# First MLP by sevens: second product ordered by the rows' arrival, rests of rows put off, second MLP's first weights split sooner, its block sums on DVE

## The chip, the cores and the metric

One core of one Trainium2 chip runs the kernel. The metric is the device time of one execution in microseconds (us), taken as the median of several runs. Engines are named as in the profile: PE (TensorE matmul), PEld (its weight load), DVE (VectorE), ACT (ScalarE), POOL (GpSimd), SP (the queue from which transfers are issued).

## What is computed

Three stages follow one another. Linear attention (4 batches, 8 heads, 576 tokens, head size 64) with a normalisation of each head; its result is a matrix x of 2304 rows and 512 columns. The first MLP has three first products whose maximum is taken. The second MLP has four experts whose results are weighted and added.

```python
def _moe_ref(x, w1, w2, w3, w_out):            # w1..w3: 512 x 768, w_out: 768 x 512
    h = np.maximum(np.maximum(x @ w1, x @ w2), x @ w3)
    return (h @ w_out).astype(np.float32)

def _moe2_ref(x, domain_probs, w1, w2):        # 4 experts, w1: 512 x 1024, w2: 1024 x 512
    p = domain_probs / (domain_probs.sum(-1, keepdims=True) + 1e-09)
    for e in range(E):
        h = np.maximum(x @ w1[e], 0.0)
        out += p[:, e:e + 1] * (h @ w2[e])
```

## The kernel before

**Split numbers.** TensorE multiplies fp32r. Every fp32 operand is kept as two fp32r parts: `hi` (a rounded copy, made by ACT) and `lo` (the rest, source minus `hi`, made by DVE in `low`, L504). A product is three matmuls, hi by hi, hi by lo and lo by hi.

**Row blocks and sevens.** The 2304 rows are six blocks of T = 384. The first MLP does block 0 and the first product of block 1 plainly (`moe1_a`, `moe1_o`). From then on two blocks go together, and a product of a 2 by 2 arrangement of blocks is done with seven block products instead of eight (`seven`, L580; six matmuls of 384 columns each). The block sums that this needs are made beforehand: `w1_sums` on the weights (four subtractions, POOL), `y_sum` on the rows (four sums, numbered 0 to 3, of 128 x 768). `w1_split`, `t_split` and `y_split` then make hi and lo of the result.

**Banks of a product.** The seven products k = 0..6 use two PSUM banks only, in the order A X A X A A X. After products 0, 2 and 4 ACT copies bank A; after 1, 4 and 6 DVE adds that copy to bank X; after 5 bank A is read again. The next product on a bank waits until it has been read.

**First MLP, units.** `units` (L620) are 18: two pairs of blocks (sb = 1, 2), three pairs of columns of the hidden layer (p), three weights (i). In a unit DVE takes the running maximum in `mx` (L661, L667), and in the last unit of three (i = 2) ACT writes the hi part of the hidden rows (L670); the lo part is handed back by `after_product1` and made by `low`. Four parts of hidden rows h[a, blk] result, in the order (0,0) after product 1, (1,1) after 4, (0,1) after 5 and (1,0) after 6. Their second product (`second1`, 48 matmuls) fills the gaps between the products of the next three units; `FILL` says how many matmuls follow each product. A block's sums with `blk` = 1 go through two banks in turn (4 and 5, evacuated by DVE L700 or ACT), those of `blk` = 0 stay in banks 0 to 3. `t_load` fetches a unit's weights two units ahead (kept in DRAM, `w_d`), POOL makes their sums, `t_split(0)` and `t_split(1)` split them after products 3 and 5 of the unit before.

**When a rest is made.** `low` puts the subtraction into a list; `lag_end` after the next product works the list off, and once more after product 5 of a unit.

**Second MLP, rounds.** 48 rounds: expert e, pair of blocks sb (3), pair of hidden columns pr (4). A round is seven products and, between them, 36 matmuls of 512 columns of the round before (`second`, L715); `store` (DVE L732) adds a finished tile to the sum. The weights of an expert are loaded, summed and split during the last four rounds of the expert before; the first expert's begin in the last units. The rows of the next pair are loaded after product 4 of pr = 0, their sums are made on POOL in pr = 1 (`y_sums`), their splits in pr = 3. In round 0 the last second product of the first MLP is the filling (`FILL_18`).

**Order.** The first stage follows a list written out by hand, `steps`: of its letters A is one product of three of block 0 or 1 with its maximum, H a split of hidden rows, P a second product, E the copies of block 0's result, Y one sum of rows, V one split of rows, R one half of `t_split`. Engines work off their queues in program order; so does SP.

## Time and profile before

| | |
|---|---|
| median of 3 runs | 1144.63 us (1143.02 to 1144.75) |
| profiled execution | 1143.08 us, its span 1141.3 us |
| PE busy | 1108.7 us, 97% of the span, 6020 matmuls |
| DVE, ACT, POOL busy | 652.8, 428.7, 274.5 us (57%, 38%, 24%) |
| mean granted TensorE clock | 0.995 of full speed |

The span is the time from the first to the last instruction. Busy time of PE counts a matmul from its start to its modelled end, and consecutive ones overlap. "Idle before" an instruction is put down to the releaser that came last.

### The profile page before, as it was taken

To read this page: it belongs to the slowest core of one execution; us is meant where nothing else is said; L and a number is where in the kernel's file an instruction comes from. 1 tells how busy PE (TensorE), PEld (TensorE's weight loads), DVE (VectorE), ACT (ScalarE), POOL (GpSimd) and SP (SyncE) were. 2 spreads that over 40 slices of the span, in tenths; PEclk is the share of its full clock that TensorE was granted. 3 is DMA by queue.
4 is the path that set the end of the run, shared out by engine and by line. 5 is a ranking of instruction groups with operands and counts; after the bars stand their busy time and mean duration, and the time that the engine had idled before them with its cause. 6 is when DMAs were issued, how large, how long until landed. Compare 5 with 4: busy or idle time off the path is not lost.

```text
span 1141.3 us, 15399 instructions
## 1 busy us (share of the span) xinstructions
PE 1108.7 (97%) x6020; PEld 1014.0 (89%) x6020; DVE 652.8 (57%) x981; ACT 428.7 (38%) x772; POOL 274.5 (24%) x244
## 2 busy tenths in 40 slices
PE   7889999999998999999999999999999999999998
PEld 6789998999998989889989888998998898999887
DVE  3889986567557564245744436583535466343523
ACT  2553233434433445243644233452424254332321
POOL 1346632422333130205220202412020522001000
PEclk9999999999999999999999999999999999999999
DMA  9945544211411412014140403432030625040111
GB/s 260 295 146 168 152 166 149 71 56 49 156 56 56 148 56 81 31 50 138 63 175 1 166 1 130 129 120 102 28 139 6 216 65 194 1 149 19 47 64 56
DMA packets 89257, 118.49 MB, mean 104 GB/s; under 512 B 11616, under 2 KB 57696, under 8 KB 89184
## 3 DMA queue, kind: packets, MB, share of 16 engines
q1 hardware_dynamic: 88480, 117.17, 32.2%
q8 instruction: 47, 0.77, 0.3%
q10 hardware_dynamic: 704, 0.33, 0.1%
q14 instruction: 26, 0.21, 0.1%
HBM read 87.59 MB, written 29.88 MB: 103 GB/s over the span
## 4 chain that ended last, share of the span: by engine, by line
PE 79%; DVE 11%; DMA 4%; ACT 2%; issue 2%; SPq 1%; POOL 1%; DVEq 0%; POOLq 0%; ACTq 0%
PE bank L586 40%; PE bank L715 35%; PE bank L683 3%; DMA w_da<-cv_a 1%; DVE ts L507 1%; DVE cv_a L232 1%; DVE ss L345 1%; DMA v<-in_v_dram 1%; DVE hr L507 1%; DVE xt L365 1%; DVE fa L659 1%; DVE fa L661 1%; DMA k<-in_k_dram 1%; DVE cv_a L235 1%; DMA w1s<-w_da 1%
## 5 line engine op out<-in xcount | busy, mean ns | idle before, releaser
L527 POOL TENSOR_TENSOR w1s<-w1s 128x256 f32<-128x256 f32 x136 | 117.1, 880 | 384.4 <-DMA w1s<-in_moe_w_dram 219.2
L611 DVE TENSOR_TENSOR fa<-bank,fa 128x384 f32<-128x384 f32 x144 | 80.1, 557 | 207.8 <-ACT fa L608 118.3
L715 PE MATMUL bank<-wr,hr 128*128 128x512 f32 x720 | 197.3, 393 | 0.0
L562 POOL TENSOR_TENSOR fa<-fa 128x768 f32<-128x768 f32 x44 | 88.4, 2020 | 289.1 <-DMA fa<-y_d 227.6
L586 PE MATMUL bank<-xr,wr 128*128 128x384 f32 x756 | 153.4, 338 | 0.0
L715 PEld LDWEIGHTS bank<-wr,hr 128*128 128x128 f32 x720 | 133.6, 188 | 17.8
L586 PEld LDWEIGHTS bank<-xr,wr 128*128 128x128 f32 x756 | 136.0, 188 | 9.7
L586 PE MATMUL bank<-rb,wr 128*128 128x384 f32 x696 | 141.3, 337 | 2.0 <-DVE hr L594 1.0
L608 ACT ACTIVATE fa<-bank 128x384 f32<-128x384 f32 x144 | 70.6, 490 | 189.8 <-PE bank L586 189.0
L586 PEld LDWEIGHTS bank<-rb,wr 128*128 128x128 f32 x696 | 125.1, 188 | 12.0 <-DVE hr L594 1.5
L715 PE MATMUL bank<-wl,hr 128*128 128x512 f32 x360 | 102.9, 394 | 0.1
L715 PE MATMUL bank<-wr,xr 128*128 128x512 f32 x288 | 93.9, 393 | 0.0
L586 PE MATMUL bank<-rb,wl 128*128 128x384 f32 x384 | 78.9, 342 | 2.4 <-DVE fa L659 2.4
L594 DVE SCALAR_TENSOR_TENSOR hr<-fa,hr 128x384 fp32r<-128x384 f32 x72 | 54.5, 757 | 42.6 <-ACT hr L593 42.6
L586 PEld LDWEIGHTS bank<-rb,wl 128*128 128x128 f32 x384 | 68.9, 190 | 7.6 <-DVE fa L659 4.0
L715 PEld LDWEIGHTS bank<-wl,hr 128*128 128x128 f32 x360 | 66.7, 188 | 9.0 <-issue 0.4
L715 PE MATMUL bank<-wr,rb 128*128 128x512 f32 x216 | 69.0, 393 | 0.0
L593 ACT ACTIVATE hr<-fa 128x384 fp32r<-128x384 f32 x72 | 37.8, 525 | 80.5 <-DVE fa L611 80.5
L593 ACT ACTIVATE xr<-fa 128x384 fp32r<-128x384 f32 x48 | 25.2, 525 | 103.1 <-DVE fa L611 103.1
L715 PEld LDWEIGHTS bank<-wr,xr 128*128 128x128 f32 x288 | 53.9, 188 | 7.9
L659 DVE TENSOR_TENSOR fa<-bank,fa 128x384 f32<-128x384 f32 x54 | 29.9, 553 | 51.0 <-ACT fa L656 36.7
L507 DVE TENSOR_TENSOR rb<-fa,rb 128x768 fp32r<-128x768 f32 (+1 forms) x45 | 43.5, 966 | 25.5 <-ACT rb L571 23.5
(170 smaller groups left out, 1789.6 us busy)
## 6 DMA issues: line engine op xcount, KB each, us to landing
fa<-y_d SPq DMA_DIRECT2D x24, 768.0 KB, 6.7
stage_a<-in_moe_w_dram SPq DMA_DIRECT2D x18, 512.0 KB, 4.1
w1s<-w_da SPq DMA_DIRECT2D x36, 256.0 KB, 2.8
o_d<-fa SPq DMA_DIRECT2D x36, 256.0 KB, 3.9
fa<-o_d SPq DMA_DIRECT2D x36, 256.0 KB, 5.3
w1s<-in_moe_w_dram SPq DMA_DIRECT2D x32, 256.0 KB, 3.1
w2s<-in_moe_w_dram SPq DMA_DIRECT2D x32, 256.0 KB, 3.2
w_da<-cv_a SPq DMA_DIRECT2D x18, 256.0 KB, 4.7
```

Of the source, the lines that this page charges most:

```text
L232: nc.vector.scalar_tensor_tensor(out=ti, in0=words[:, :, 0], scalar=29, in1=ti, op0=ALU.logical_shift_right, op1=ALU.bitwise_or)
L507: nc.vector.tensor_tensor(out=lo, in0=src, in1=f32(hi), op=ALU.subtract)
L527: eng.tensor_tensor(out=st[:, o], in0=st[:, a], in1=st[:, b], op=ALU.subtract)
L562: eng.tensor_tensor(out=y_part(o), in0=y_part(a), in1=y_part(b), op=op)
L586: nc.tensor.matmul(out, w[wi][:, c * P : (c + 1) * P], y[yi][:, c, :], start=(i == 0 and k in BEGIN), stop=(i == 5), skip_group_check=k no ...
L593: nc.scalar.activation(out=h[0], in_=src, func=AF.Relu)
L594: nc.vector.scalar_tensor_tensor(out=h[1], in0=src, scalar=0.0, in1=f32(h[0]), op0=ALU.max, op1=ALU.subtract)
L608: nc.scalar.activation(out=s[k // 2], in_=a, func=AF.Copy)
L611: nc.vector.tensor_tensor(out=t, in0=x, in1=t, op=ALU.add)
L659: nc.vector.tensor_tensor(out=mx[done] if i == 0 else t, in0=x, in1=t, op=ALU.add)
L683: nc.tensor.matmul(bank[:, :T], w[:, wi, c * P : (c + 1) * P], h[a, blk][hi], start=((blk == 1 or p == 0) and a == 0 and n == 0), stop=((b ...
L715: nc.tensor.matmul(banks[i], h[a, i // TPB][hi][:, i % TPB * P : (i % TPB + 1) * P], w[a][wi], start=(pr == 0 and a == 0 and m == 0), stop ...
```

## The change

The second product of the first MLP takes its parts in another order: all of (blk 0, a 0), then blk 1, then (blk 0, a 1). A rest of hidden rows is made 2 to 4 products later instead of one (`by`), through a list with due times (`lag_at`). In a unit `t_split(1)` stands ahead of `after_product1` at product 5. The first sums of rows stand earlier in `steps`. The second MLP's first weights (e = 0, pr = 0) have a place of their own (`w1e`) and are loaded in unit 10, summed in unit 12 on POOL and split in units 13 and 15, instead of loaded in unit 16 and split in unit 17; the next ones (pr = 1) take the load in unit 16. In the second MLP the four sums of rows go from POOL (pr = 1) to DVE (pr = 2, one after each of products 0 to 3). The copies of the last block 4 are all on ACT, and `FILL_18` is redistributed. Rests in round 0 are put off by a product as well.

```diff
--- before.py
+++ after.py
@@ -431,7 +431,7 @@
     def y_put(j, c, bank, t):
-        if c % 2:
+        if c % 2 and j < 4:
             nc.vector.tensor_copy(out=t, in_=bank)
         else:
             nc.scalar.activation(out=t, in_=bank, func=AF.Copy)
@@ -463,14 +463,14 @@
     FILL = [(0, 2, 1, 2, 2, 5, 2, 2), (0, 2, 1, 2, 2, 5, 2, 2), (0, 2, 1, 2, 2, 5, 2, 2)]
     FILL_0 = [(0, 0, 1, 0, 1, 4, 1, 1)] * 3
     FILL_9 = [(0, 4, 4, 3, 3, 4, 2, 2), (0, 1, 2, 1, 2, 4, 2, 1), (0, 1, 2, 1, 2, 4, 2, 1)]
-    FILL_18 = (0, 8, 6, 6, 6, 8, 7, 7)
+    FILL_18 = (0, 8, 8, 10, 10, 6, 3, 3)
     SPLIT = {(8, 1): (0,), (8, 2): (1,), (8, 4): (2,), (8, 6): (3,), (0, 0): (4,), (0, 2): (5,), (0, 3): (6,)}
     bank_of = {"A": banks[7], "X": banks[6]}
     wr = []
     late = {}
-    lag = [None]
+    lag = {"now": None, "put": []}
     first = [1]
     def y_at(k):
@@ -501,35 +501,45 @@
         return first, second
-    def low(lo, src, hi):
-
-        if lag[0] is None:
+    def low(lo, src, hi, by=1):
+
+        if lag["now"] is None:
             nc.vector.tensor_tensor(out=lo, in0=src, in1=f32(hi), op=ALU.subtract)
         else:
-            lag[0].append((lo, src, hi))
-
-    def lag_end(again=None):
-        put, lag[0] = lag[0] or [], None
-        for p in put:
-            low(*p)
-        lag[0] = again
-
-
-    def w1_load(e, pr):
-        st = late["w1"].rearrange("p (n c f) -> p n c f", n=8, f=P)
+            lag["put"].append((lag["now"] + by, (lo, src, hi)))
+
+    def lag_at(now):
+
+        put, lag["put"], lag["now"] = lag["put"], [], None
+        for due, args in put:
+            if now is None or due <= now:
+                low(*args)
+            else:
+                lag["put"].append((due, args))
+        lag["now"] = now
+
+
+    def w1_at(early):
+
+        if early:
+            return late["w1e"], part(fa, 7 * HK + 3 * T, 4 * 2 * P)
+        return late["w1"][:, : 4 * 2 * P], late["w1"][:, 4 * 2 * P :]
+
+    def w1_load(e, pr, early=False):
+        st = w1_at(early)[0].rearrange("p (n c f) -> p n c f", n=4, f=P)
         for at, f in ((0, pr + NPR), (2, pr)):
             src = e_w1[e, :, f * P : (f + 1) * P].rearrange("(c p) f -> p c f", p=P)
             nc.sync.dma_start(out=st[:, at : at + 2].rearrange("p n c f -> p (n c) f"), in_=src)
-    def w1_sums(eng):
-        st = late["w1"].rearrange("p (n f) -> p n f", n=8)
+    def w1_sums(eng, early=False):
+        st = [t[:, n * 2 * P : (n + 1) * 2 * P] for t in w1_at(early) for n in range(4)]
         for o, a, b in ((4, 0, 2), (5, 1, 4), (6, 1, 0), (7, 3, 5)):
-            eng.tensor_tensor(out=st[:, o], in0=st[:, a], in1=st[:, b], op=ALU.subtract)
-
-    def w1_split(pr, half):
+            eng.tensor_tensor(out=st[o], in0=st[a], in1=st[b], op=ALU.subtract)
+
+    def w1_split(pr, half, early=False):
         cols = slice(0, 3 * 2 * P) if half == 0 else slice(3 * 2 * P, 7 * 2 * P)
         (hi, lo), _ = w_slot(pr)
-        src = late["w1"][:, 2 * P :][:, cols]
+        src = w1_at(early)[half][:, 2 * P if half == 0 else 0 :]
         nc.scalar.activation(out=hi[:, cols], in_=src, func=AF.Copy)
         low(lo[:, cols], src, hi[:, cols])
@@ -673,19 +683,19 @@
     def second1(sb, p):
         h = h_of((sb - 1) * NPF + p + 1)
-        for blk in (1, 0):
-            for c in range(KD):
-                bank = banks[4 + c % 2] if blk else banks[c]
-                for a in range(2):
-                    w = wt["o", 0, p + a * NPF]
-                    for n, (wi, hi) in enumerate(((0, 0), (1, 0), (0, 1))):
-                        last = (a, n) == (1, 2)
-                        nc.tensor.matmul(
-                            bank[:, :T], w[:, wi, c * P : (c + 1) * P], h[a, blk][hi],
-                            start=((blk == 1 or p == 0) and a == 0 and n == 0),
-                            stop=((blk == 1 or p == NPF - 1) and last),
-                        )
-                        yield (blk, c) if last else None
+
+        parts = [(0, c, 0) for c in range(KD)] + [(1, c, a) for c in range(KD) for a in range(2)]
+        for blk, c, a in parts + [(0, c, 1) for c in range(KD)]:
+            bank = banks[4 + c % 2] if blk else banks[c]
+            w = wt["o", 0, p + a * NPF]
+            for n, (wi, hi) in enumerate(((0, 0), (1, 0), (0, 1))):
+                last = (a, n) == (1, 2)
+                nc.tensor.matmul(
+                    bank[:, :T], w[:, wi, c * P : (c + 1) * P], h[a, blk][hi],
+                    start=((blk == 1 or p == 0) and a == 0 and n == 0),
+                    stop=((blk == 1 or p == NPF - 1) and last),
+                )
+                yield (blk, c) if last else None
     def rest1(sb, p, blk, c):
         if blk == 0:
@@ -830,7 +840,7 @@
             "A012 A112 d13 c14 d14 A212 s12.pp A202 s13.av s14.vv A102 H12.pv c15 P1 H02 A003.v d15 c16 c17 "
             "A013 A113 d16 d17 A203 A103 s15.pp c18 A213 H03 s16.pv H13.pv d18 s17 s18.vv c19 d19 c20 d20 "
             "s19.pv A004 A014 A104 c21 s20.av c22 P2 A204 A114 d21 W H04 d22 c23 s21.pv s22.av A214 P3 "
-            "A005.v H14 A015.v d23 s23.av Z A205 P4 V0 A105 H05 R0 V1 A215 Y0 A115 H15 P5 E Y1 V3 Y2 V4 R1 "
+            "A005.v H14 A015.v d23 s23.av Z A205 Y0 P4 V0 Y1 A105 Y2 H05 R0 V1 A215 A115 H15 P5 E V3 V4 R1 "
             "Y3 V6"
         ).split()
         for st in steps:
@@ -881,6 +891,7 @@
                 cv_cm.__exit__(None, None, None)
                 lp = ctx.enter_context(tc.tile_pool(name="late", bufs=1, reuse_waits="tile"))
                 late["o"] = lp.tile([P, 2, DM], F32, name="ob")
+                late["w1e"] = lp.tile([P, 4 * 2 * P], F32, name="w1e")
                 late["w1"] = lp.tile([P, 8 * 2 * P], F32, name="w1s")
                 t_cm = tc.tile_pool(name="tp", bufs=1, reuse_waits="tile")
                 late["t"] = t_cm.__enter__().tile([P, 2 * 4 * 2 * P], F32R, name="ts")
@@ -937,25 +948,31 @@
             go(fill, first)
             for k in range(7):
                 product1(u, k)
+                if k == 5 and u + 1 < len(units):
+                    t_split(1)
                 put = after_product1(u, k)
-                lag_end([])
+                lag_at(7 * u + k)
                 if put:
-                    low(*put)
+                    low(*put, by={1: 2, 4: 3, 5: 2, 6: 4}[k])
                 go(fill, after[k])
                 if u + 1 < len(units):
                     if k == 3:
                         t_split(0)
                     if k == 5:
-                        t_split(1)
-                        lag_end([])
+                        lag_at(7 * u + 6)
                         if u + 2 < len(units):
                             t_load(u + 2)
                         else:
-                            w1_load(0, 0)
+                            w1_load(0, 1)
                         w1_sums(nc.gpsimd)
-                elif k in (1, 3):
-                    w1_split(0, k // 2)
+
+                if (u, k) == (10, 6):
+                    w1_load(0, 0, True)
+                if (u, k) == (12, 0):
+                    w1_sums(nc.gpsimd, True)
+                if (u, k) in ((13, 4), (15, 4)):
+                    w1_split(0, u // 15, True)
                 if (u, k) in ((0, 6), (9, 6)):
                     y_load(*((2, x_d) if sb == 1 else (0, None)))
                 if (u, k) == (3, 6):
@@ -966,8 +983,7 @@
                     y_sum(nc.vector, (3, 4, 6, 7).index(u % 9))
                 for n in SPLIT.get((u % 9, k), ()) if u > 7 else ():
                     y_split(n)
-        lag_end()
-        go(fill, 99)
+        assert not any(fill)
         t_cm.__exit__(None, None, None)
         late["w2"] = ctx.enter_context(tc.tile_pool(name="w2p", bufs=1, reuse_waits="tile")).tile([P, 2, DM], F32, name="w2s")
@@ -982,12 +998,13 @@
         for e in range(E):
             for pr in range(NPR):
                 n = (e * NSB - 1) * NPR + pr
-                w1_at, w2_at = (n + 1, n + 2) if e else (pr - 1, pr)
-                if w1_at >= 0:
-                    at(w1_at - 1, 3 if e else 5, w1_load, e, pr)
-                    at(w1_at - 1, 3 if e else 5, w1_sums, nc.gpsimd)
+                w1_by, w2_at = (n + 1, n + 2) if e else (pr - 1, pr)
+                if e or pr > 1:
+                    at(w1_by - 1, 3 if e else 5, w1_load, e, pr)
+                    at(w1_by - 1, 3 if e else 5, w1_sums, nc.gpsimd)
+                if e or pr:
                     for i in range(2):
-                        at(w1_at, (1 if e or pr == 1 else 4) + i, w1_split, pr, i)
+                        at(w1_by, (1 + i if e else 2 + i if pr == 1 else 4 + i), w1_split, pr, i)
                 at(w2_at - 1, 6, w2_load, e, pr)
                 for i in range(2):
                     at(w2_at, 3 + 2 * i, w2_split, pr, i)
@@ -998,7 +1015,6 @@
         before = None
         fill = second_of(*units[-1][:2])
-        run(-1, 5)
         run(-1, 6)
         go(fill, FILL_18[0])
         for n, (e, sb, pr) in enumerate(rounds):
@@ -1012,6 +1028,7 @@
                 product(pr, k)
                 after_product(n, k)
                 if n == 0:
+                    lag_at(7 * len(units) + k)
                     go(fill, FILL_18[1 + k])
                     for i in SPLIT.get((0, k), ()):
                         y_split(i)
@@ -1023,14 +1040,15 @@
                 if more:
                     if pr == 0 and k == 4:
                         y_load((sb + 1) % NSB)
-                    if pr == 1 and k == 3:
-                        y_sums(nc.gpsimd)
+                    if pr == 2 and k < 4:
+                        y_sum(nc.vector, k)
                     if pr == NPR - 1:
                         y_split(k)
                 if e and pr == 1 and k == 4:
                     o_load(sb)
                 run(n, k)
             before = (e, sb, pr)
+            lag_at(None)
         for i in second(n, pr):
             if i is not None:
                 store(e, sb, i)
```

## Rows read from the trace of the kernel before

**Rows 1.** Windows: us; busy us (x) PE, PEld, DVE, ACT, POOL; PEclk; DMA; GB/s.

```profile
176.60:367.00 190.40, 184.92 (x1023) 177.24 (x1022) 120.55 (x198) 75.72 (x144) 61.59 (x73) 1.00 0.25 80
367.00:388.50 21.50, 18.89 (x98) 18.24 (x96) 18.02 (x27) 10.77 (x19) 3.69 (x4) 0.92 0.32 110
388.50:410.00 21.50, 19.48 (x94) 16.82 (x95) 12.08 (x12) 6.83 (x13) 13.50 (x11) 1.00 0.48 158
410.00:1128.00 718.00, 718.00 (x3565) 646.14 (x3564) 354.11 (x498) 265.98 (x469) 122.64 (x90) 1.00 0.25 85
```

**Rows 2.** Waits of PE from 176.6 to 410 us: total us, times, longest.

```profile
PE bank L683 <- DVE hr L507: 3.0, 2, 2.6
PE bank L586 <- ACT fa L656: 2.6, 5, 1.1
PE bank L586 <- DVE fa L659: 2.4, 5, 0.6
PE bank L586 <- DVE hr L594: 1.0, 1, 1.0
PE bank L586 <- DVE fa L611: 0.9, 1, 0.9
```

**Rows 3.** Timeline at unit 0: start, us, instruction, idle before and its releaser.

```profile
179.85 0.49 ACT L656 ACTIVATE fa<-bank 128x384 f32<-128x384 f32 x1 [1.38 <-DVE op L507]
180.40 1.43 PE L586 MATMUL bank<-rb,ts 128*128 128x384 f32 x6 [1.11 <-ACT fa L656]
```

**Rows 4.** Timeline from the end of unit 2 into unit 3.

```profile
204.61 1.22 PE L586 MATMUL bank<-xr,wr 128*128 128x384 f32 x6
...
205.39 1.23 DVE L507 TENSOR_TENSOR hr<-fa,hr 128x384 fp32r<-128x384 f32 x2
...
206.59 0.69 DVE L507 TENSOR_TENSOR ts<-w1s,ts 128x512 fp32r<-128x512 f32 x1
...
207.20 0.55 DVE L659 TENSOR_TENSOR fa<-bank,fa 128x384 f32<-128x384 f32 x1
...
207.80 1.32 PE L586 MATMUL bank<-rb,wl 128*128 128x384 f32 x6 [0.39 <-DVE fa L659]
207.83 4.36 POOL L527 TENSOR_TENSOR w1s<-w1s 128x256 f32<-128x256 f32 x4 [4.31 <-DVE fa L659]
```

**Rows 5.** Timeline from unit 8 into unit 9.

```profile
273.80 0.83 ACT L571 ACTIVATE xr<-fa 128x768 fp32r<-128x768 f32 x1
...
275.06 1.15 PE L586 MATMUL bank<-rb,ts 128*128 128x384 f32 x5 [0.40 <-ACT fa L656]
```

**Rows 6.** Timeline of unit 17 and round 0.

```profile
362.10 1.32 PE L586 MATMUL bank<-xr,ts 128*128 128x384 f32 x6 [0.73 <-ACT fa L656]
...
370.11 1.08 DVE L507 TENSOR_TENSOR hr<-fa,hr 128x384 fp32r<-128x384 f32 x1
...
371.24 2.15 PE L683 MATMUL bank<-hr,wr 128*128 128x384 f32 x6 [2.59 <-DVE hr L507]
```

**Rows 7.** Timeline of round 1 into round 2.

```profile
397.31 8.41 POOL L562 TENSOR_TENSOR fa<-fa 128x768 f32<-128x768 f32 x4
...
401.42 2.60 DVE L507 TENSOR_TENSOR wr<-w1s,wr 128x768 fp32r<-128x768 f32 x1
...
404.55 1.32 PE L586 MATMUL bank<-rb,wr 128*128 128x384 f32 x6 [1.05 <-DVE hr L594]
...
407.92 1.31 PE L586 MATMUL bank<-rb,wr 128*128 128x384 f32 x6 [0.91 <-DVE fa L611]
```

**Rows 8.** Groups of DVE and POOL from 410 to 1128 us: busy us, mean ns, idle before.

```profile
L507 DVE TENSOR_TENSOR wl<-w1s,wl 128x768 fp32r<-128x768 f32 (+1 forms) x6 | 13.7, 2315 | 1.2 <-ACT wl L533 1.2
```

**Rows 9.** Groups over the whole span (matmuls of sevens, sums of weights and rows).

```profile
L586 PE MATMUL bank<-xr,wr 128*128 128x384 f32 x756 | 153.4, 338 | 0.0
...
L527 POOL TENSOR_TENSOR w1s<-w1s 128x256 f32<-128x256 f32 x136 | 117.1, 880 | 384.4 <-DMA w1s<-in_moe_w_dram 219.2
L562 POOL TENSOR_TENSOR fa<-fa 128x768 f32<-128x768 f32 x44 | 88.4, 2020 | 289.1 <-DMA fa<-y_d 227.6
...
L562 DVE TENSOR_TENSOR fa<-fa 128x768 f32<-128x768 f32 x12 | 11.5, 962 | 0.0
```

## The prediction, made before the change was run

> **What bounds the kernel now.** I read first the windows by stage [rows 1]. From 410 to 1128 us PE is busy for all of 718.00 us: this stretch is PE's own work, none of the edits takes a matmul away, and so nothing can be won there, only lost. What can be won lies before 410 us. In the units (176.6 to 367) PE lacks 190.40 - 184.92 = 5.48 us, in the handover to the second MLP (367 to 388.5) 2.61 us, in rounds 1 and 2 (388.5 to 410) 2.02 us: 10.1 us. The list of PE's waits over that stretch accounts for 9.9 us of it in 14 waits, all behind ACT or DVE, none behind a transfer [rows 2]. Two things are to be added. A wait costs more than its gap, since matmuls overlap: six take 1.22 us [rows 4] and one lasts 0.338 [rows 9], so the pitch is 0.176 and a restart loses another 0.16; 14 of them are 2.2 us. And in the handover the granted clock has a mean of 0.92 where all other stretches have 1.00 [rows 1]: for a part of it PE ran at the lower of its two levels, 1.2 instead of 2.4 GHz, and 0.08 x 21.5 = 1.7 us were lost; six matmuls that follow the gap of 2.59 us take 2.15 us there [rows 6] against 1.22. The ceiling of the change is 9.9 + 2.2 + 1.7 = 13.8 us. PE being dense behind, what is won before 410 us reaches the end in full.
>
> **The change part by part, each against its own stall.** The unit is us, gap plus 0.16.
>
> *Sums of rows earlier.* At 180.40 product 2 of unit 0 waits 1.11 us for the copy of bank A, and that copy stands behind DVE's rest of a rows' split, for which ACT waited 1.38 us [rows 3]. The edit changes no count: three sums of 0.96 us [rows 9] move to a place where DVE waits for PE and for transfers anyway. The same queue then reaches the late splits about 1.5 us sooner. Against it: the maximum after A105 now stands behind two of the sums, so H05, which P5 needs, is up to 1.5 us later. I count 1.1 of 1.27 as won (bounds: loss of 1.5, gain of 1.3).
>
> *Rests put off, order by arrival, t_split(1) first.* From unit 2 into 3 PE's product 6 ends at 205.83, but the addition that frees bank X starts only at 207.20: ahead of it DVE makes two rests of hidden rows (1.23 together) and the rest of t_split (0.69) [rows 4]. After the change only the 0.69 stands there, and it starts sooner since ACT no longer has it behind the hidden rows; the addition comes right behind the product. The two rests go behind product 0 of the next unit, where DVE has 1.4 us (product 1 and two matmuls of filling) until it is needed for bank X. Their first reader allows it: the order now begins with h[0,0], whose rest is made inside unit i = 2, and reaches h[0,1] at matmul 12 instead of 0, h[1,0] at 36. This takes the five "DVE fa L659" waits (2.4), the small DVE wait of second1 (3.0 - 2.59 = 0.4) and the small ACT waits at product 2 (2.6 - 1.11 - 0.73 = 0.8): 3.6, and with 9 restarts 5.0. Not all of it: at unit 9 ACT still has a split of rows (0.83) ahead of the bank's copy [rows 5], 0.6 stays, and 0.4 for sums on POOL that now run closer to these additions. I count 4.0 (bounds 1 and 5).
>
> *First weights of the second MLP split in units 13 and 15.* Unit 17 loses ACT and DVE work of two splits; product 4 there waits 0.73 us for a bank copy that stands behind splits on ACT [rows 6]. One split of rows stays ahead, so 0.7 of 0.89. In units 13 and 15 the work meets engines that are busy 63% (DVE) and 40% (ACT) [rows 1], behind product 4, with the next bank addition two products away: nothing. The load in unit 10 is one of many, and the early POOL sums of unit 12 are four times 0.88 [rows 9] on an engine busy for a third; nothing.
>
> *The handover.* The 2.59 us at 371.24 is a wait for the rest of h[0,1] [rows 6]. That rest took 1.08 us beside POOL's weight sums and had a rows' split and a bank addition ahead of it. In the new order the first 12 matmuls of filling read only h[0,0], whose rest is long made, and FILL_18 gives 16 matmuls before the first that needs h[0,1]. The gap goes, 2.75, and the clock with it, since it fell only behind this gap: 1.7. Together 4.4 (bounds 2 and 4.4).
>
> *Given back at the end of round 0.* In the handover DVE is busy 18.02 of 21.5 us [rows 1]. Without 4.4 us of idle and slow PE only 17.1 remain. Two copies (1.1, a pass over a bank being 0.55 [rows 4]) go to ACT, and some 1.5 of contention with POOL's sums (an estimate: three rests at half as much again, as the one of 1.08) go too, since these now run in unit 16 to 17; that leaves 15.4 in 17.1, in a queue that also waits for ACT's hi parts. The rests of rows, two rests of weights and the rest of h[1,0], each put off by a product, collect behind products 3 and 4, ahead of the read of bank A after product 5, for which product 0 of round 1 waits. I work out that this read ends about 1 us late: -1.0 (bounds 0 and -4).
>
> *Block sums on DVE.* In round 1 a rest of weights took 2.60 us, while POOL ran four sums of 8.41 us in all; PE then waited 1.05 and 0.91 us for additions behind it [rows 7]. With the sums gone from POOL such a rest takes about 1 us, and both waits go: 2.3 with restarts. The price is 44 sums x 0.96 = 42 us more on DVE [rows 9]. It is hidden by PE: DVE is busy 354 of 718 us and becomes busy 396, or 55% [rows 1]. That there is slack to take a late DVE is shown by the rests of weights in this stretch that took 2.3 us on average beside POOL [rows 8], without one wait of PE. The sum after product 1 stands behind the bank addition and two products (over 3 us) ahead of the next need of that bank; its input was loaded more than a round before. POOL loses 88 us, on no path: nothing.
>
> The Trainium skill ("SBUF — State Buffer", Who interferes with whom) says that a DVE instruction with two SBUF inputs and a GpSimd one that reads SBUF exclude each other for a whole instruction. The 2.60 us agree with it: one wait for a POOL sum of 2.1. By that rule the sums' move is worth more than its 42 us suggest, but it also speaks against the transitions between units, as the first rival.
>
> **The sum.** 1.1 + 4.0 + 0.7 + 4.4 - 1.0 + 2.3 = 11.5 us. The profiled execution took 1143.08 us, so 1131.6. The median of the runs is 1.55 above that execution, and of three runs two lay there and one at 1143.02; I add 0.9 and say 1132.5.
>
> **The rivals.**
>
> *POOL takes the transitions back.* POOL's four subtractions start when t_split(1) has been read, and that is now 1.3 us sooner, against a maximum and two rests on DVE, each with two inputs in SBUF. If each waits for a whole subtraction (0.88) [rows 9], the addition of product 1 comes 0.9 us late in each of five transitions: 4.4 back, 1136.5. For it: POOL's four took 4.36 instead of 3.5 in one transition [rows 4], both sides lose. Against: the rest beside POOL at 370.11 took 1.08 [rows 6] instead of about 0.6 [rows 4], half a subtraction more, and then the slack holds.
>
> *Round 0 becomes DVE's.* If contention does not fall and handshakes with ACT cost more, DVE's 18 us are the length of the round: 3.4 more given back than counted, 1136. For it: the 84% of now. Against: 1.5 us of them is contention.
>
> *It does not do what it says.* The transitions are then set by the chain of weights (load, POOL sums, ACT split), which would take the place of the rests; round 0 shifts its wait into round 1. Only the 2.3 of the sums and some of the head would stay, less the give-back: 1142. Against: no PE wait in [rows 2] is behind a transfer or POOL.
>
> *Slower.* The sums on DVE delay the bank additions in pr = 2. The point where this decides: DVE more than two products behind at an addition. If half of the 44 sums stood exposed, 22 x 0.96 = 21 us would be lost, 1153 in the end; a dozen exposed eat the whole gain. For it: in the last pair of rows two rests of weights and two of the second product stand in the same round. Against: the slow rests of [rows 8] stood there too, and PE did not wait.
>
> **How the numbers follow.** A measurement of this kernel can tell about 0.2%, 2.3 us. Forecast 0.57, POOL rival 0.13, round 0 rival 0.13, no effect 0.09, slower 0.08. Faster is the first three and a little of the fourth, 0.84; same 0.08; slower 0.08. The likeliest case alone reaches from 1129 (the ceiling) to 1136; the range takes in both middle rivals and leaves out the slower case and most of no effect: 1128.5 to 1140.5.
>
> **What would show it.** In the new trace: no gap of PE behind the additions L659 at the five transitions; second1's first matmuls in round 0 without a wait and a granted clock of 1.00 there; at most 1 us of gap at product 0 of round 1; no gap at 404 and 408 and the rests of weights at about 1 us; no wait of PE in the rounds behind, with DVE near 55%. Gaps of about 1 us in every round with pr = 2, or a new wait near P5, would prove me wrong.

## The result and the profile after

| | before | after |
|---|---|---|
| median | 1144.57 us (4 runs, 1143.02 to 1144.75) | 1132.39 us (4 runs, 1132.06 to 1133.07) |
| ratio | | 0.9897 [0.988, 0.9915] |
| profiled execution, its span | 1143.08, 1141.3 us | 1132.06, 1130.3 us |

The forecast was 1132.5 us, and the working for the profiled execution 1131.6. The page of the kernel after begins so (busy time, share of the span, instructions):

```profile
span 1130.3 us, 15358 instructions
PE 1104.6 (98%) x6020; PEld 1012.8 (90%) x6020; DVE 667.6 (59%) x1023; ACT 429.3 (38%) x774; POOL 189.5 (17%) x200
```

The windows by stage, columns as in [rows 1]: from the first matmul of the units to their end, the handover (round 0), round 1, and all that follows up to 1117 us.

```profile
177.50:361.50 184.00, 182.14 (x1022) 177.45 (x1021) 122.50 (x197) 74.13 (x142) 66.37 (x76) 1.00 0.27 83
361.50:378.00 16.50, 16.09 (x92) 15.59 (x90) 14.05 (x23) 10.40 (x19) 0.00 (x0) 1.00 0.31 103
378.00:394.80 16.80, 16.09 (x78) 14.19 (x79) 7.96 (x12) 6.64 (x12) 3.31 (x4) 1.00 0.55 190
394.80:1117.00 722.20, 722.20 (x3586) 649.91 (x3586) 374.38 (x546) 267.12 (x471) 44.87 (x52) 1.00 0.25 85
```

PE lacks 1.86 us in the units where it lacked 5.48, and the handover has a granted clock of 1.00 where it had 0.92. In the last window PE is busy throughout, though DVE's share there went from 49% (354.11 of 718.00) to 52%. What is left of PE's waits from 177.5 to 396 us (in all, times, longest) is 3.1 us in 6 waits, against the 9.9 in 14 of [rows 2]:

```profile
PE bank L596 <- DVE fa L669: 1.2, 2, 0.6
PE bank L725 <- ACT fa L437: 0.7, 1, 0.7
PE bank L596 <- ACT fa L666: 0.7, 2, 0.4
PE bank L596 <- DVE hr L604: 0.5, 1, 0.5
```

**Stage by stage.** PE issues the same 2772 matmuls of sevens in both kernels, so a stage can be measured on PE alone: the length of a unit or round is the time from the first matmul of its product 0 to the first of the next one's, both read from the timeline. The first row starts at the last matmul of block 1's first products (L259); ahead of it only three sums of rows have another place and one load starts later. The last row ends at the start of the last matmul of sevens.

| stage | before | after | difference | term of the prediction |
|---|---|---|---|---|
| up to unit 0 | 11.05 | 12.12 | +1.07 | head |
| unit 0 | 10.54 | 8.91 | -1.63 | head: -1.1 in all |
| units 1 to 16 | 168.41 | 164.56 | -3.85 | transitions: -4.0 |
| unit 17 | 11.30 | 10.52 | -0.78 | -0.7 |
| round 0 | 20.19 | 16.53 | -3.66 | handover -4.4, part of the +1.0 |
| round 1 | 17.28 | 16.79 | -0.49 | sums: half of -2.3, rest of the +1.0 |
| round 2 | 16.98 | 15.69 | -1.29 | sums: the other half |
| rounds 3 to 47 | 706.17 | 706.15 | -0.02 | 0 |

The column adds up to -10.65; the spans differ by 11.0, and the 0.35 that is missing lies ahead of the first row. A stage's length mostly repeats to 0.1 to 0.35 us between executions: unit 0 is 8.91 here and in nine kernels below, the rounds from 3 on 706.15 to 706.18 in eleven, and in both kernels above; units 1 to 16 are 164.21 to 164.56 in kernels that differ only elsewhere. (A stretch with a lower clock, as in round 0 of the kernel before, changes more.) The time at which unit 0 starts varies more (177.52 us here, 180.24 in a kernel below that changes nothing ahead of it). So an experiment can be read from its stages even where its median can't tell.

### The profile page after: what moved, and what is told of

It is laid out like the page before. It is cut to its first block, busy times and chain, and to the rows that moved or that the text cites. A ratio compares the mean times of both kernels' runs of the same rounds, so it can differ in the third digit from the quotient of the medians.

```text
span 1130.3 us, 15358 instructions
## 1 busy us (share of the span) xinstructions
PE 1104.6 (98%) x6020; PEld 1012.8 (90%) x6020; DVE 667.6 (59%) x1023; ACT 429.3 (38%) x774; POOL 189.5 (17%) x200
## 4 chain that ended last, share of the span: by engine, by line
PE 82%; DVE 8%; DMA 3%; issue 2%; POOL 1%; ACT 1%; SPq 1%; DVEq 0%; POOLq 0%; ACTq 0%
PE bank L596 41%; PE bank L725 35%; PE bank L693 4%; DMA w_da<-cv_a 1%; PE bank L423 1%; DVE cv_a L232 1%; DMA w1s<-w_da 1%; DMA k<-in_k_dram 1%; DVE cv_a L235 1%; DVE cv_a L231 1%; DMA q<-in_q_dram 1%; DVE fa L404 1%; DVE ss L345 0%; DVE xt L365 0%; DVE cv_o L232 0%
## 5 line engine op out<-in xcount | busy, mean ns | idle before, releaser
L604 DVE SCALAR_TENSOR_TENSOR hr<-fa,hr 128x384 fp32r<-128x384 f32 x72 | 43.8, 608 | 42.6 <-ACT hr L603 42.6
L572 DVE TENSOR_TENSOR fa<-fa 128x768 f32<-128x768 f32 x56 | 53.3, 964 | 0.3
```

The costliest lines, as they stand in the source:

```text
L572: eng.tensor_tensor(out=y_part(o), in0=y_part(a), in1=y_part(b), op=op)
L604: nc.vector.scalar_tensor_tensor(out=h[1], in0=src, scalar=0.0, in1=f32(h[0]), op0=ALU.max, op1=ALU.subtract)
```

## Experiments

Each kernel is the one after, or the one before, with the edit shown. Ratios are to the kernel before in runs on the same chip. The kernel before had a median of 1144.15 us beside four of them (sums back on POOL, old order, rests soon, weights late), 1142.87 beside four more (`t_split(1)` late, head in the old order, sums twice, the first mended kernel) and 1144.9 beside the last four (sums alone, order alone, the new tile's place, the second mended kernel).

### The block sums back on POOL

```diff
-                    if pr == 2 and k < 4:
-                        y_sum(nc.vector, k)
+                    if pr == 1 and k == 3:
+                        y_sums(nc.gpsimd)
```

> The changed kernel with the block sums of the second MLP back on POOL in pr = 1, all else as changed. My theory (POOL's sums slow DVE's rests in round 1, and PE waits for bank additions behind them): the rests of weights in round 1 take 2 to 2.6 us again, PE waits about 1 us twice at the start of round 2, 2.3 us more than the changed kernel, near 1134.5. Rival (DVE is ahead by now since the handover is lighter, so a slow rest is taken by slack): no wait, 1132.4. Against the kernel before: -10 or -12 us.

1134.99 us, ratio 0.9918 [0.9902, 0.9935]. Round 2 takes 19.69 us instead of 15.69, and every other stage from unit 0 on is within 0.1 of the kernel after. Timeline of rounds 1 and 2 in this kernel:

```profile
390.52 8.90 POOL L572 TENSOR_TENSOR fa<-fa 128x768 f32<-128x768 f32 x4
...
393.13 2.35 DVE L507 TENSOR_TENSOR wr<-w1s,wr 128x768 fp32r<-128x768 f32 x1 [0.17 <-ACT wr L543]
...
397.66 2.84 DVE L507 TENSOR_TENSOR wr<-w1s,wr 128x1024 fp32r<-128x1024 f32 x1
...
400.43 0.55 DVE L621 TENSOR_TENSOR fa<-bank,fa 128x384 f32<-128x384 f32 x1
...
401.03 2.29 PE L596 MATMUL bank<-rb,wr 128*128 128x384 f32 x6 [2.33 <-DVE fa L621]
```

The two waits of [rows 7] come back as one of 2.33 us, behind DVE's rest of 2.84. That a wait returns is as expected, its size is not: 4.0 us are lost in this profile, where the two waits and their restarts were 2.3. The rest is a slow stretch: the six matmuls behind the gap take 2.29. The windows before, of and behind it (columns as above):

```profile
400.70:404.10 3.40, 3.07 (x9) 2.88 (x10) 1.80 (x3) 0.99 (x3) 3.03 (x4) 0.51 0.01 4
404.10:410.00 5.90, 5.90 (x31) 5.34 (x30) 1.25 (x2) 1.45 (x3) 0.00 (x0) 1.00 0.17 44
```

PE ran at the lower of its two levels (1.2 GHz) for 3.4 us. This profiled execution is the slowest of the four (1137.56 us); the other three lie at 1134.35 to 1135.04, 2.0 to 2.7 above the kernel after, which is the gap without the slow stretch.

### The sums alone, in the kernel before

```diff
-                    if pr == 1 and k == 3:
-                        y_sums(nc.gpsimd)
+                    if pr == 2 and k < 4:
+                        y_sum(nc.vector, k)
```

> The kernel before with the block sums of the second MLP on DVE as its one change. My theory: the two waits at the start of round 2 (1.05 and 0.91) go, and nothing else moves: 2.3 us less than the kernel before, with no wait of PE behind 410 us. Rival (the gain of 4.0 that the other way round showed is the sums' own): 4 us less. The difference, as I see it, is the granted clock: before, the two gaps lay apart and the clock stayed up.

1140.27 us (8 runs), ratio 0.997 [0.9956, 0.9983]. Rounds 1 and 2 take 16.06 and 15.69 us instead of 17.28 and 16.98: 2.5 gained. The ratio stands for more, 3.4 us (1.9 to 5.0), but rounds 1 to 47, which the sums can reach, are no more than 2.5 shorter; so the rival of 4 falls. Of the two parts that were run alone this is the one that works by itself. Round 0 is shorter too, by 1.54, though none of its work differs. Its wait is there as in [rows 6], with the first line below; but the window that begins with it has the full clock:

```profile
371.57 0.62 PE L683 MATMUL bank<-hr,wr 128*128 128x384 f32 x2 [2.59 <-DVE hr L507]
```

```profile
368.90:373.00 4.10, 1.51 (x9) 1.43 (x9) 4.07 (x7) 2.37 (x4) 2.20 (x2) 1.00 0.01 4
```

In the kernel before, the window behind that gap reads

```profile
371.24:374.80 3.56, 3.56 (x12) 3.56 (x13) 2.70 (x4) 1.35 (x3) 0.00 (x0) 0.53 0.17 60
```

So the 1.7 us of clock in the prediction are real in the execution that it was read from, and not a sure part of the kernel before.

### Twice the sums on DVE

```diff
-                        y_sum(nc.vector, k)
+                        for _ in range((3, 1, 2, 2)[k]):
+                            y_sum(nc.vector, k)
```

The 44 further sums write the same values again.

> The changed kernel with 44 block sums more on DVE in the second MLP: sum 0 made three times, sums 2 and 3 twice, all with the same result; 42 us of DVE work added. My theory (DVE has slack in every round): within 0.5 us of the changed kernel, no wait of PE in the rounds. Rival (the sums stand close to the bank additions, and the next one shows): 0.3 us or more in each of 11 rounds, 4 us or more, up to 42.

1134.12 us, ratio 0.9924 [0.9908, 0.994]; 0.3 more in round 2 and 0.5 in all rounds from 3 on. DVE's group of sums in this kernel, over the units and rounds:

```profile
L572 DVE TENSOR_TENSOR fa<-fa 128x768 f32<-128x768 f32 x96 | 91.9, 964 | 1.8
```

Some 42 us more DVE work cost 0.8 us of PE's time. The slower rival of the prediction, DVE sums that stand exposed, is excluded with room to spare.

### The old order of the second product

`second1` and `FILL_18` as before, all else as after.

```diff
-        parts = [(0, c, 0) for c in range(KD)] + [(1, c, a) for c in range(KD) for a in range(2)]
-        for blk, c, a in parts + [(0, c, 1) for c in range(KD)]:
...
+        for blk in (1, 0):
+            for c in range(KD):
...
+                for a in range(2):
...
-    FILL_18 = (0, 8, 8, 10, 10, 6, 3, 3)
+    FILL_18 = (0, 8, 6, 6, 6, 8, 7, 7)
```

> The changed kernel with the old order of the second product (blk 1 first) and the old FILL_18; rests are still put off. My theory: the order matters where many matmuls follow product 0, at unit 9 and above all in round 0, where the rest of h[0,1] is needed at the third matmul: 1 to 2 us of wait at round 0, about 1 us at unit 9, none elsewhere, 1.5 to 3 us more than the changed kernel. Rival (the order is what the gap of 2.59 us hung on, with the clock behind it): 3.5 us or more come back, with a granted clock under 1 in round 0. Second rival (putting off and lighter engines did it all): no difference.

1139.09 us, ratio 0.9961 [0.9946, 0.9975]: my theory, that the order matters at unit 9 and in the handover alone, falls. The first line of its PE waits:

```profile
PE bank L694 <- DVE hr L507: 6.5, 6, 2.8
```

The units 1 to 16 take 171.40 us, 6.8 more than after and 3 more than before; unit 9 alone loses 3.05, with a fallen clock behind its gap (last section). PE comes to rests that are put off by 2 to 4 products before they are made, and waits, in six places: at all five transitions and in round 0.

### Order and filling alone, in the kernel before

The same edit the other way round, into the kernel before.

> The kernel before with the new order of the second product and the new FILL_18 alone; rests as before. My theory: the gap of 2.59 us in the handover goes with the clock behind it, 4.4, of which round 0 gives 1 to 2 back since DVE and POOL are as loaded as before; the transitions between column pairs keep their waits behind bank additions and lose only the 0.4 behind the rest: 2.5 to 4 us less than the kernel before. Rival (order, putting off and the place of t_split need one another everywhere): under 1.5 us.

1146.96 us (9 runs), ratio 1.0022 [1.001, 1.0034]: a little slower, where I expected 2.5 to 4 less. That theory falls too. Its waits of PE, from unit 0 into round 2:

```profile
PE bank L586 <- DVE fa L659: 3.4, 5, 1.2
PE bank L586 <- ACT fa L656: 3.4, 7, 1.1
PE bank L586 <- DVE fa L611: 2.6, 1, 2.6
PE bank L682 <- DVE fa L699: 2.0, 1, 2.0
PE bank L714 <- DVE fa L435: 1.4, 1, 1.4
```

The five waits behind L659 are there still, since the rests still stand ahead of the addition; those into units 9 and 12 are longer, which makes 3.4 in all for the 2.4 of [rows 2]. The new ones of 2.0 and 1.4 are for evacuations of the last blocks' banks on DVE; why DVE is late there was not pursued. Units 1 to 16 lose 2.0 us and round 2 loses 1.65; round 0 takes 18.32, less than the 20.19 before, but hardly less than the 18.65 of the kernel with the sums alone, whose clock stayed up. In round 2 the two waits of [rows 7] come as one of 2.6 (L611), as with the sums on POOL.

### Rests made soon, and `t_split(1)` late

Two kernels, each the one after with one of the two moves undone.

```diff
-                    low(*put, by={1: 2, 4: 3, 5: 2, 6: 4}[k])
+                    low(*put)
```

> The changed kernel with every rest of hidden rows made one product later, as before, not 2 to 4; order and t_split(1) as changed. My theory: the two rests stand ahead of the bank addition again; PE waits 0.3 to 0.8 us at each of the five transitions between column pairs, 2 to 3.5 us more than the changed kernel. Rival (moving t_split(1) ahead is what freed DVE): under 0.5 us more.

```diff
-                if k == 5 and u + 1 < len(units):
-                    t_split(1)
...
                     if k == 5:
+                        t_split(1)
                         lag_at(7 * u + 6)
```

> The changed kernel with t_split(1) back behind the filling of product 5; rests put off and order as changed. My theory: with the two rests gone its own rest (0.69) still fits ahead of the bank addition, but comes 1 us later, and POOL's sums with it: 0 to 1.5 us more than the changed kernel. Rival (this move is what freed the transitions): 2 us or more.

1138.0 us (0.9947 [0.9932, 0.9962]) and 1137.46 us (0.9957 [0.994, 0.9974]). Units 1 to 16 take 168.61 and 168.48 us: each loses 4 us, and each by itself gives back the whole gain of the transitions (before: 168.41). For the first I expected 2 to 3.5, for the second at most 1.5, and there my theory falls. From unit 2 into 3 the kernel with the late split reads:

```profile
204.78 1.21 PE L596 MATMUL bank<-xr,wr 128*128 128x384 f32 x6
...
206.10 0.61 ACT L647 ACTIVATE ts<-w1s 128x512 fp32r<-128x512 f32 x1
...
206.75 0.69 DVE L507 TENSOR_TENSOR ts<-w1s,ts 128x512 fp32r<-128x512 f32 x1 [1.11 <-ACT ts L647]
...
207.35 0.55 DVE L669 TENSOR_TENSOR fa<-bank,fa 128x384 f32<-128x384 f32 x1
```

ACT makes the hi part only behind the hidden parts, DVE waits 1.11 us for it, and the addition starts 2.57 us after product 6 did, as late as in [rows 4] (2.59). So order, putting off and split gain nothing in units 1 to 16 when one of the three is missing; putting off alone and the split alone were not run. Round 0 is not like that: it takes 16.54 and 16.53 us in these two kernels, as in the kernel after.

### The first weights of the second MLP late

Loaded in unit 16 and split in unit 17, the next ones loaded behind the units, as before.

```diff
-                            w1_load(0, 1)
+                            w1_load(0, 0)
...
-                if (u, k) == (10, 6):
-                    w1_load(0, 0, True)
-                if (u, k) == (12, 0):
-                    w1_sums(nc.gpsimd, True)
-                if (u, k) in ((13, 4), (15, 4)):
-                    w1_split(0, u // 15, True)
+                if u == len(units) - 1 and k in (1, 3):
+                    w1_split(0, k // 2)
...
-                if e or pr > 1:
+                if e or pr:
...
+        run(-1, 5)
```

> The changed kernel with the first weights of the second MLP loaded in unit 16 and split in unit 17, and the next ones loaded behind the units, as before. My theory: the wait at unit 14 (about 0.8 with its restart) goes, that of 0.9 at unit 17 comes back, and the handover gains 0.5 to 1.5 us of waits because DVE has two rests more and POOL's sums beside it: 0.5 to 2 us more than the changed kernel. Rival (the handover's gap was DVE's load, and the order alone does not help): 3 us or more.

1134.76 us, ratio 0.9915 [0.9899, 0.9931]. Unit 17 loses 1.06 us (11.58 for 10.52) and round 0 0.86, while units 1 to 16 gain 0.65: 0.87 in unit 14, less 0.26 in unit 10. Net 1.3, inside the expected 0.5 to 2, and the 0.87 is a cost of the change that the prediction did not have.

### The head in the old order

```diff
-... A205 Y0 P4 V0 Y1 A105 Y2 H05 R0 V1 A215 A115 H15 P5 E V3 V4 R1 ...
+... A205 P4 V0 A105 H05 R0 V1 A215 Y0 A115 H15 P5 E Y1 V3 Y2 V4 R1 ...
```

> The changed kernel with the sums of rows at their old places in the hand-written order. My theory: the wait at product 2 of unit 0 comes back (1.3 with restart), the new waits behind P5 (0.45 and 0.5 of 0.8) go: 0.3 to 0.9 us more than the changed kernel. Rival (the move pays its full 1.1 of the prediction): 1.1 us or more.

1134.5 us, ratio 0.9932 [0.9912, 0.9951]. Unit 0 takes 10.56 us again (8.91), so the sums' place is worth 1.65 there. But the stretch ahead of unit 0 is 12.00 us, no shorter than the 12.12 after, against 11.05 before: the new order of the steps is not what made that stretch longer.

### The new tile behind the old one in memory

In the kernel after, the new tile `w1e` is allocated ahead of `w1s`, so `w1s` lies elsewhere than before. Here the two change places.

```diff
-                late["w1e"] = lp.tile([P, 4 * 2 * P], F32, name="w1e")
                 late["w1"] = lp.tile([P, 8 * 2 * P], F32, name="w1s")
+                late["w1e"] = lp.tile([P, 4 * 2 * P], F32, name="w1e")
```

> The changed kernel with the new tile for the first weights allocated behind the tile of the weights in work, not ahead of it. My theory (the first load of weights waits for the last user of the memory under it, and the new tile moved it onto memory that DVE frees 1.1 to 1.4 us later): the first load starts right behind the last conversion again, and PE is 0.9 us sooner at unit 0 counted from the last first product of block 1. Rival (the waits there come from the sums of rows ahead of the maxima): no change.

1131.97 us, ratio 0.9897 [0.9881, 0.9913]. The stretch up to unit 0 falls from 12.12 to 11.30 us, as expected (0.9). In the kernel after, the first load of `w1s` (SP, L642) is issued right behind DVE's last subtraction from `cv_o`, a working tile of the stage ahead (159.13 + 0.69 = 159.82); later PE waits for the copies that come behind the late split (timeline of after):

```profile
159.13 0.69 DVE L209 TENSOR_TENSOR wr<-cv_o,wr 128x512 fp32r<-128x512 f32 x1 [0.70 <-ACT wr L69]
159.90 0.80 SPq L642 DMA_DIRECT2D w1s<-w_da  x2
...
169.18 0.80 PE L423 MATMUL bank<-op,wl 128*128 128x384 f32 x3 [0.29 <-DVE fa L404]
...
171.16 0.80 PE L423 MATMUL bank<-op,wl 128*128 128x384 f32 x3 [0.65 <-ACT fa L437]
```

In the kernel before the same load does not wait for that subtraction, and was issued ahead of it:

```profile
158.84 0.80 SPq L632 DMA_DIRECT2D w1s<-w_da  x2
159.47 0.69 DVE L209 TENSOR_TENSOR wr<-cv_o,wr 128x512 fp32r<-128x512 f32 x1 [0.70 <-ACT wr L69]
```

So it is again in the kernel with the other allocation:

```profile
160.90 0.79 SPq L642 DMA_DIRECT2D w1s<-w_da  x2
...
161.53 0.69 DVE L209 TENSOR_TENSOR wr<-cv_o,wr 128x512 fp32r<-128x512 f32 x1 [0.70 <-ACT wr L69]
```

### What is left mended

The kernel after with the first half of the first weights split in unit 12 instead of 13, the splits of rows 3 and 4 one product later at unit 9, `E` ahead of `H15`, and FILL_18 moved towards product 5. The second kernel adds the allocation above, one more split of rows moved, and half of the next weights split in unit 17.

```diff
-    FILL_18 = (0, 8, 8, 10, 10, 6, 3, 3)
+    FILL_18 = (0, 8, 8, 10, 10, 8, 4, 0)
...
+    SPLIT_9 = {(8, 1): (0,), (8, 2): (1,), (8, 4): (2,), (0, 0): (3,), (0, 1): (4,), (0, 2): (5,), (0, 3): (6,)}
...
-... A115 H15 P5 E V3 ...
+... A115 P5 E H15 V3 ...
...
-                if (u, k) in ((13, 4), (15, 4)):
+                if (u, k) in ((12, 4), (15, 4)):
...
-                for n in SPLIT.get((u % 9, k), ()) if u > 7 else ():
+                for n in (SPLIT_9 if 8 <= u < 17 else SPLIT).get((u % 9, k), ()) if u > 7 else ():
```

> The changed kernel with its remaining waits mended: the first weights' half 0 split in unit 12 instead of 13 (a unit without a maximum), FILL_18 given out by product 5, so that the last copy of block 4 stands ahead of the last hidden part, block 0's copies ahead of H15, and at unit 9 the splits of rows 3 and 4 one product later. My theory: unit 14 gives 0.85, round 1 0.8, the head 0.5, unit 9 0.5: 2 to 2.7 us less than the changed kernel, near 1130. Rival (the waits only move on, since DVE is full in round 0 and at unit 9): less than 0.7 us.

```diff
-... (8, 4): (2,), (0, 0): (3,) ...
+... (8, 3): (2,), (0, 0): (3,) ...
...
+                if (u, k) == (17, 4):
+                    w1_split(1, 0)
...
-                    for i in range(2):
-                        at(w1_by, (1 + i if e else 2 + i if pr == 1 else 4 + i), w1_split, pr, i)
+                    for i in range(0 if e or pr > 1 else 1, 2):
+                        at(w1_by, (1 + i if e else 1 + i if pr == 1 else 4 + i), w1_split, pr, i)
```

> The mended kernel with three things more: the new tile behind the old one, the third split of rows of unit 8 one product sooner, and half 0 of the weights of pr = 1 split in unit 17 instead of round 0. My theory: the waits at unit 9 (0.77) and at product 0 of round 1 (0.7) go, and the head gives 0.2: 1.2 to 1.7 us less than the mended kernel from unit 0 on. Rival (they only move on): under 0.4 us less.

1130.72 us (0.9893 [0.9876, 0.9911]) and 1129.53 us (0.9875 [0.9859, 0.989]). The first takes 1.74 us out of units 1 to 16, 0.95 out of round 1 (15.84 for 16.79), whose wait for a copy is gone, and 0.97 out of the stretch up to unit 0 (11.15 for 12.12), by `E` ahead of `H15`, its only edit there: 3.7 us from the head to the last seven. The second adds 0.5 to that, all of it ahead of unit 0; from unit 0 on, where most of the expected 1.2 to 1.7 should have come, it gains nothing. Two waits go, but unit 8 gets 0.6 longer and a new wait of 0.54 appears in round 0, so here the rival holds: they only move on. From 166 us to 1118 PE is now busy 951.09 of 952.00 us, so PE's listed idle time in these stages is below 1 us:

```profile
166.00:1118.00 952.00, 951.09 (x4858) 871.92 (x4856) 529.34 (x792) 365.50 (x655) 119.49 (x135) 1.00 0.26 87
```

## Why the prediction was right, step by step

The terms were forecast to add up to 11.5 us and were 10.6 in the profiled execution, which took 1132.06 us and not 1131.6. That the median comes within 0.1 us of the forecast is luck: 0.9 was added for the spread of the runs where 0.33 came (1132.39 for 1132.06), and that cancels the 0.5 by which the profiled execution missed its working.

**Sums of rows earlier: 1.1 forecast, 0.56 measured.** Unit 0 won more than was counted (1.63; a kernel with the same unit 0 as before took 10.20 there, so up to 0.35 of it may be variation), and for the loss ahead of it the step took off only 0.17. There 1.07 was lost, with new waits behind P5 (0.29 and 0.65, above), which the prediction had named as a sign of being wrong. The bound of 1.5 for it was argued from the queue on DVE behind A105; the runs show another cause, the place of the new tile in memory (0.8 of the 1.07, by the kernel with the other allocation; the old order of the steps gave nothing back). A diff that adds a tile moves other tiles, and this part of the change was not costed.

**Transitions: 4.0 forecast, 3.85 measured, by two errors that cancel.** The waits at four of the five transitions are gone; into unit 9 0.61 and 0.40 are left. From product 6 of unit 2 into unit 3, the kernel after reads:

```profile
203.48 1.22 PE L596 MATMUL bank<-xr,wr 128*128 128x384 f32 x6
...
204.39 0.69 DVE L507 TENSOR_TENSOR ts<-w1s,ts 128x512 fp32r<-128x512 f32 x1
...
205.00 0.55 DVE L669 TENSOR_TENSOR fa<-bank,fa 128x384 f32<-128x384 f32 x1
...
206.53 0.55 DVE L507 TENSOR_TENSOR hr<-fa,hr 128x384 fp32r<-128x384 f32 x1
```

The addition starts 1.5 us after product 6 did, where it was 2.6 [rows 4], with only the rest of `t_split` ahead of it; the first rest of hidden rows comes 1 us behind it. That is the chain as it was forecast, and it gave more than was counted: units 3, 6, 9, 12 and 15, which begin with the transitions, are 5.1 us shorter. Against it stands the step that failed: the early split of the first weights in units 13 and 15 was costed at nothing, since the engines are busy 63% and 40% there. From unit 13 into 14:

```profile
318.54 2.15 POOL L537 TENSOR_TENSOR w1s<-w1s 128x256 f32<-128x256 f32 x2 [5.16 <-DVE ts L507]
...
318.79 1.30 DVE L507 TENSOR_TENSOR wl<-w1e,wl 128x768 fp32r<-128x768 f32 x1
...
320.01 1.23 DVE L507 TENSOR_TENSOR ts<-w1s,ts 128x512 fp32r<-128x512 f32 x1
...
321.16 0.54 DVE L669 TENSOR_TENSOR fa<-bank,fa 128x384 f32<-128x384 f32 x1
...
321.76 0.44 PE L596 MATMUL bank<-rb,wl 128*128 128x384 f32 x1 [0.59 <-DVE fa L669]
```

The new rest (1.30) and that of `t_split` (1.23 where it is 0.69 alone) stand in one line ahead of the addition, both beside POOL's subtractions, and PE waits 0.59; unit 14 gets 0.86 longer. (The other units lose 0.37 in all.) Late weights and the mended kernel both take this back (0.87). The share of an engine over 190 us said nothing about the 2.5 us ahead of one addition; in unit 12 the same work costs 0.13 (unit 13 takes 10.34 for 10.21).

**Unit 17: 0.7 forecast, 0.78 measured,** and 1.06 comes back with the late split.

**The handover: 4.4 forecast, 4.3 measured.** No wait is listed for `second1` and the clock is 1.00. (Round 0's 3.66 is this less the 0.62 below.) Of the 4.4 the 2.75 is the wait; the 1.7 of clock belongs to the profiled execution and not to each one, as the sums alone showed: against that kernel's round 0 (18.65) the kernel after wins 2.12, with the 0.62 2.74, the wait alone. In how many executions of the kernel before the clock fell there is not known. A slip of the working had no effect: not 16 but 12 matmuls of filling stand ahead of the first that needs h[0,1].

**Given back at the end of round 0: 1.0 forecast, 1.45 measured, from two causes of which one was forecast.** At the end of round 0 and in round 1, after:

```profile
376.31 1.22 DVE L507 TENSOR_TENSOR wr<-w1s,wr 128x1024 fp32r<-128x1024 f32 x1
...
377.45 0.55 DVE L604 SCALAR_TENSOR_TENSOR hr<-bank,hr 128x384 fp32r<-128x384 f32 x1
...
378.05 1.34 PE L596 MATMUL bank<-rb,wr 128*128 128x384 f32 x6 [0.46 <-DVE hr L604]
...
379.10 0.52 ACT L603 ACTIVATE hr<-fa 128x384 fp32r<-128x384 f32 x1 [2.12 <-DVE fa L621]
379.52 0.47 ACT L437 ACTIVATE fa<-bank 128x384 f32<-128x384 f32 x1
```

The first is the one that was worked out: product 0 of round 1 waits for the read of bank A (L604) behind a rest of weights, 0.46 and a restart, 0.62. The second is the copy of the last block's bank, which the diff moved from DVE to ACT: it stands on ACT behind the last hidden part, and the second product that needs the bank waits 0.66 us at 380.05 for it, 0.83 with what follows. The copies were counted as relief of DVE only, not by what they queue behind on ACT. In the mended kernel this second wait is gone.

**Block sums on DVE: 2.3 forecast, 2.6 measured** (1.29 in round 2, and 1.32 in round 1, whose 0.49 is net of the 0.83). Alone in the kernel before they gave 2.5. The group of rests of weights of [rows 8] went to a mean of 1.1 us, without a wait of PE:

```profile
L507 DVE TENSOR_TENSOR wl<-w1s,wl 128x768 fp32r<-128x768 f32 (+1 forms) x6 | 6.6, 1093 | 3.0 <-ACT wl L543 3.0
```

DVE's share behind 394.8 us is 52% and not the 55% of the forecast. The 44 sums add 41.9 us, but without POOL's sums beside them other instructions of DVE take about 21 less: these rests 6.6 for 13.7, hidden parts from a tile (hr<-fa, 69 of them) a mean of 610 ns for 743. That relief was not counted.

**The rivals.** *POOL takes the transitions back* was half right: the two rests above took 1.30 and 1.23 us instead of 0.96 and 0.69. But this decided at one transition, into unit 14, where a second rest stood in the line; the 4.4 of five did not come. The Trainium skill ("SBUF — State Buffer", Who interferes with whom) has it that two such instructions contend for one read interface under an exclusive lock, and that the order of issue decides which of them is blocked. The sums on POOL agree, with rests of 2.35 and 2.84 us beside sums of about 2.2 (0.96 and 1.22 alone), and so do the transitions, where a rest lost 0.34 and 0.54, less than a mean subtraction on POOL takes (0.88 in [rows 9]). *Round 0 becomes DVE's* came as 0.62 of its 3.4. *No effect* is out by the stages. *Slower through the sums* is out by twice the sums.

## What to carry to other kernels

An order by arrival, a postponed producer and a cleared queue ahead of a bank's evacuation are one change: here two without the third lost 4 to 7 us in the units, and the order alone made the kernel before slower. Cost work that is moved "into slack" at the next evacuation behind it on the same in-order engine, not by the engine's share over the stage. A new tile also moves its neighbours in memory, and a load that used to be free may then wait for the last reader of another tile.

## What the hardware showed that was not expected

The granted clock's answer to a gap of PE was not the same from one execution to the next. After gaps of 2.33 us (sums on POOL, 0.51 for 3.4 us), 2.59 (before, 0.53 for 3.6) and 2.79 (old order, 0.53 for 3.6) PE ran near 1.2 GHz; after the same 2.59 in the kernel with the sums alone, and after 2.02 and 2.56 in the kernel with the order alone, it stayed at 2.4 (a granted clock of 1.00 from 179 to 430 us). What tells these cases apart stays open. In the old order it reads:

```profile
272.40:276.00 3.60, 3.60 (x13) 3.60 (x13) 1.60 (x3) 0.61 (x1) 0.00 (x0) 0.53 0.02 5
```
